# Top-k attention and a gated MLP on one core: the first 25 slots issued in an order from a table, six gates and twelve small additions moved to GpSimd

## The chip, the cores and the metric

The kernel runs on one core of a Trainium2 chip. The metric is the device time of one execution in microseconds. The core has five instruction queues that run side by side, each strictly in the order in which the program lists it: TensorE (PE; its weight loads are shown apart as PEld), VectorE (DVE), ScalarE (ACT), GpSimd (POOL) and SyncE (SP), which here issues nearly all transfers. Engines wait for each other through semaphores.

## The reference

Attention over 8 batches of 8 heads, 576 rows of 64, in which each row keeps its 32 largest scores; its output, 4608 rows of 512, goes through a dense block of width 2048 with a gate.

```python
scores = scale * np.matmul(q, k.transpose(0, 1, 3, 2))
kth = np.partition(scores, -32, axis=-1)[..., -32:-31]
scores = np.where(scores >= kth, scores, -1e9)
attn = np.exp(scores - np.max(scores, axis=-1, keepdims=True))
attn = attn / (np.sum(attn, axis=-1, keepdims=True) + 1e-09)
x = np.matmul(attn, v)            # then (B, H, S, D) -> (B*S, H*D)
h = x @ w_in
out = (h * (1.0 / (1.0 + np.exp(-1.702 * h)))) @ w_out
```

q, k and v are float32; w_in and w_out come as float64.

## The kernel before

**Slots.** The attention is cut into 144 slots of 128 rows by two heads (or four heads' last 64 rows), 18 to a batch. A slot runs through these steps, each a function of the kernel:

- `scores` (L330): eight matmuls on PE into the only score buffer in PSUM, `s_ps`. `copy_scores` (L345): ACT copies them to `sc`, of which there are four buffers.
- `pair_up` (L354): DVE writes the larger and the smaller of each two scores to `ranked`. `topk` (L374): four rounds of MAX8 and MATCH_REPLACE8 on DVE find the 32 largest. Since `pair_up` empties the score buffer together with `copy_scores`, it stands in the middle of the ranking of the slot before.
- `bounds` (L399): POOL makes `cut` and `low` from `top`. `mask` (L414) and `exps` (L422) on ACT give `pr` and the sums `den`. `invert` (L433): 1e-9 is added to `den` (on DVE up to slot 11, on POOL from slot 12, because of `n > PAIRED`), and DVE takes the reciprocal `rden`.
- The probabilities are transposed. Up to slot 9 PE does it, with a diagonal matrix `by` that POOL makes from `rden` (`divide` L443, `turn` L458). From slot 10 on POOL normalizes `pr` (L450), ACT splits it into halves of words in `sc` (`split` L486), SP writes them to `rows` in DRAM and reads them back transposed into `pt` (`turn_by_dma` L494).
- `values` (L515, L548, L566): matmuls of `v` with `pt`, 64 output rows at a time, the two heads side by side in the array; ACT copies the result to `xT`.

**Blocks.** Four slots make a block of 128 rows for the dense part; there are 36. Each is worked off in four units: `hidden` (L651) is the matmul with w_in; `tanh` (L673) is ACT's; `gate` (L685) multiplies; `combine` (L702) makes sums for the seven products that `project` (L755) multiplies with w_out. The first two blocks (`whole`) are done without such sums. `tanh(aside)` chooses the gate's engine: with `False` one DVE instruction reads the hidden values from PSUM; with `True` ACT first copies them to `h` in SBUF, and POOL takes two instructions.

**Weights.** The 32 pieces of w_in and w_out arrive as float64 and are made float32 during slots 0 to 10, by steps of `round_piece` (L136) on ACT (`size`, `sign`, `low`), DVE (`shift`) and POOL (`finish`, `pool_size`). PE gets dummy matmuls from `stay_warm` (L170) in slots with little to do.

**Order.** All order is written by hand, and the issue order of the program is each engine's order. `opening` (L907) begins; `slot` (L949) does slots 0 to 10; `filling_slot` (L1099), called by `filling` (L1138), does 11 to 20 with lists of extra work; `steady_pair` (L1175) does two slots at a time from 21 on; `last_units` (L1241) works off the dense units that are left. Loads of v are `load_v` (L208): v has one buffer, so the load for the next batch waits for the last values of this one.

Of the kernel before, what the change touches and what calls it, by code (L numbers as in the profile page):

```python
# [9 lines left out]
ALU = mybir.AluOpType  # L10
# [19 lines left out]
TO_ZERO = 2.0**-100  # L30


@with_exitstack
def kernel(
    ctx: ExitStack,
# [23 lines left out]

    nc = tc.nc

    B, H, S, D = q.shape
    C = H * D
# [23 lines left out]
    PAIRED = SETTLED + 1  # L89
    STEADY = PAIRED + 2  # L90
# [25 lines left out]
    both_banks = [ps_p.tile([P, 512], F32, name=f"po{i}") for i in range(2)]  # L116

    ident = const.tile([P, P], F32, name="ident")
    make_identity(nc, ident[:])
    win = const.tile([P, CC, DFF], F32, name="win")  # L120
    wout = const.tile([P, FC, C], F32, name="wout")

# [199 lines left out]
    N = len(slots)  # L322
    PER = N // B
    st = [{} for _ in slots]
# [83 lines left out]
    def exponentials(n, between=lambda: None):  # L408

        mask(n)  # L410
        between()
        exps(n)
# [20 lines left out]
    def invert(n):  # L433

        some = small.tile([P, 2], F32, name="some", tag="sums")
        if n > PAIRED:
            nc.gpsimd.tensor_scalar(some[:], st[n]["den"][:], 1e-9, None, op0=ALU.add)  # L437
        else:
            nc.vector.tensor_scalar_add(some[:], st[n]["den"][:], 1e-9)
        rden = st[n]["rden"] = small.tile([P, 2], F32, name="rden", tag="inverse")  # L440
        nc.vector.reciprocal(rden[:], some[:])  # L441

# [190 lines left out]
    class Block:  # L633
        def __init__(self, place, rows):
            self.place, self.rows = place, rows
            self.whole = len(blocks_seen) < WHOLE
            self.bank = 1 - len(blocks_seen) % 2
            blocks_seen.append(self)
            self.left = list(range(FC))
            if not self.whole:  # L640
                self.left = [h * (FC // 2) + 2 * u + c for u in range(4) for h in range(2) for c in range(2)]
            self.done = 0
# [30 lines left out]
    def tanh(aside):  # L673

        if to_gate:
            ph, fs, x = to_gate.pop(0)
            th = thp.tile([P, G * P], F32, name="th")
            nc.scalar.activation(th[:], ph, AF.Tanh, scale=0.851 / RAISE)
            if aside:
                h = thp.tile([P, G * P], F32, name="h", tag="th")  # L680
                nc.scalar.copy(out=h[:], in_=ph)  # L681
                ph = h[:]
            gated.append((th, ph, fs, x, aside))
# [161 lines left out]
    for n in by_slot:  # L845
        first = sum(map(len, list(by_slot.values())[:n]))
# [60 lines left out]
    def opening():  # L907

        stay_warm(8, v_tail[:, 0, :, :].rearrange("p j d -> p (j d)"))
        load("q", 0, 0, nc.sync)  # L910
        load("k", 0, 0, nc.scalar)
        for hp in range(2):
            for name in "qk":
                if hp:
                    load(name, 0, hp)
        for x in by_slot[0]:
            load_piece(x)
        prepare_first()
# [30 lines left out]
    def slot(n):  # L949

        todo = later.pop(n, [])
        for fn, args in todo:
            if fn not in (prepare, prepare_by_dma, load_piece):
                fn(*args)
        preparing = [(fn, args) for fn, args in todo if fn is prepare or fn is prepare_by_dma]
        some = [round_piece(x) for x in by_slot.get(n, [])] if n else early
        steps = {name: [piece[name] for piece in some] for name in ("size", "shift", "low")}
        last = some[-1] if len(some) > 2 else None
        if last:
            steps["size"].pop()  # L960

        def do(name, count):
            for _ in range(min(count, len(steps[name]))):
                steps[name].pop(0)()

        if n == 0:
            steps["size"].clear()
            do("low", 3)
        else:
            exponentials(n - 1, bring_all if n % 4 == 1 and n > TURNS + 1 else lambda: None)  # L970
            if n == TURNS + 1:
                stay_warm(14)
                bring_all()
            copy_scores(n + 1)
            bring_all()
            if 1 < n <= TURNS:
                turn_main(n - 2)
                turn_ends(n - 2)
            if n > TURNS + 1:
                tanh(False)  # L980
            do("size", 3)
            if n == TURNS + 1:
                do("low", 3)
                tanh(False)
        for i, op in enumerate(topk(n)):
            op()
            if i == 1:
                for _ in range(min(3, len(unfinished))):
                    finish_one()
                if last and n > 2:  # L990
                    last["pool_size"]()
            if i == (9 if n < 3 else 7):
                if n > 0:
                    divide(n - 1)
                if last and n < 3:
                    last["pool_size"]()
# [36 lines left out]
        if n > PROJECTS and may_project(2):  # L1033
            project(n == SETTLED)
        if idle:
            stay_warm(8)
        if n == SETTLED:
            turn_qk(1, 0)
        hidden()
# [59 lines left out]
    def filling_slot(n, beside, pool_ahead, behind, pool_behind, late=[]):  # L1099

        todo = later.pop(n, [])
        due = [(fn, args) for fn, args in todo if fn is prepare_by_dma]
        exponentials(n - 1)
        for fn in beside:
            fn()
        for fn in pool_ahead:
            fn()
        find(n, 8)
        for fn, args in todo:
            if fn is load_v:  # L1110
                fn(*args)
        scores(n + 2)
        if n == PAIRED:
            normalize(n - 1)
            split(n - 1)
            copy_scores(n + 2)
        else:
            copy_scores(n + 2)
            normalize(n - 1)
            split(n - 1)  # L1120
        write_all()
        for fn, args in todo:
            if fn not in (prepare_by_dma, load_v):
                fn(*args)
        turn_by_dma(n - 1)
        while turns:
            turns.pop(0)()
        for fn in pool_behind:
            fn()
        bounds(n)  # L1130
        for fn in behind + late:
            fn()
        for fn, args in due:
            fn(*args)
# [106 lines left out]
    def last_units():  # L1241
# [7 lines left out]
        project_one()  # L1249
        leave_all()  # L1250

    with tc.manual_schedule():
        opening()
        for n in range(SETTLED + 1):
            slot(n)
        filling()
        for n in range(STEADY + 8, N + 2, 2):
            steady_pair(n)
        combine()
        while ready or to_gate or gated or to_combine or to_project:  # L1260
            last_units()
        merge_some(len(merging), nc.vector)
        write_all()
# [30 lines left out]
```

## Time and profile before

| | us |
|---|---|
| median of three runs (lowest, highest) | 1379.32 (1377.34, 1382.84) |
| the profiled execution's own time | 1379.59 |
| its span | 1377.8 |
| busy: PE, DVE, ACT, POOL | 1341.2, 1286.0, 1164.1, 964.4 |
| mean granted TensorE clock | 0.992 |

The span runs from the first to the last instruction that the profiler recorded; the time is a little longer than it. Busy time is the time in which an engine had an instruction under way; for PE the ends of matmuls are modelled, and a float32 matmul shows as two records. A row of the groups gives line, engine, operation, output and inputs with their shapes, the count, then busy us, the mean of one in ns, the idle time before them and what ended it. `POOL by L448` is the instruction on POOL that writes `by` at line 448. A row of the timeline gives start, length, and what ran, with equal neighbours merged (x4 is four).

### The profile page before, as it was taken

How to read it: one execution, taken by the hardware profiler on the slowest of the kernel's cores; microseconds unless marked ns; L12 is line 12 of the kernel's file. 1: busy time of each engine (PE TensorE's matmuls, PEld its weight loads, DVE VectorE, ACT ScalarE, POOL GpSimd, SP SyncE). 2: the span in 40 equal slices, each digit the busy share in tenths (PEclk: the TensorE clock that was granted, in tenths of full speed). 3: DMA queues.
4: the chain of work that ended last, by engine and by line, in shares of the span. 5: the costliest groups of instructions: out<-in, count | busy, mean ns of one | idle time of the engine just before them, and what ended most of it. 6: DMA issues, size and time to landing. Idle time of an engine off the chain costs nothing.

```text
span 1377.8 us, 54398 instructions
## 1 busy us (share of the span) xinstructions
PE 1341.2 (97%) x22560; PEld 1205.0 (87%) x22560; DVE 1286.0 (93%) x3392; ACT 1164.1 (84%) x1930; POOL 964.4 (70%) x1758
## 2 busy tenths in 40 slices
PE   7789999999999999999999999999999999999998
PEld 5676578899999999999999999999998999999998
DVE  7999998999999999999999999999999999999912
ACT  6988887998889888988898988888888998888841
POOL 3776676777777776777777777677777777777770
PEclk8999999999999999999999999999999999999999
DMA  7551568787889786977898668988888768855640
GB/s 232 155 163 62 151 159 198 179 196 196 205 210 211 178 189 173 232 193 192 192 227 208 182 174 193 210 198 191 197 211 208 195 176 183 184 142 135 151 118 17
DMA packets 527223, 246.92 MB, mean 179 GB/s; under 512 B 458880, under 2 KB 505472, under 8 KB 526976
## 3 DMA queue, kind: packets, MB, share of 16 engines
q1 hardware_dynamic: 526544, 243.16, 71.5%
q8 instruction: 177, 2.90, 0.9%
q14 instruction: 70, 0.57, 0.1%
q10 hardware_dynamic: 432, 0.30, 0.1%
HBM read 46.01 MB, written 103.42 MB: 108 GB/s over the span
## 4 chain that ended last, share of the span: by engine, by line
PE 79%; DMA 3%; ACT 1%; issue 0%; POOL 0%; SPq 0%; DVE 0%; DVEq 0%; ACTq 0%; POOLq 0%
PE ph L662 32%; PE po L776 28%; PE o L586 10%; PE s_ps L339 9%; DMA pt<-rows 2%; DMA rows<-sc 1%; ACT pr L428 0%; ACT sc L418 0%; ACT sc L490 0%; ACT sc L350 0%; ACT halves L268 0%; ACT raws L794 0%; SPq L221 0%; POOL pr L454 0%; ACT h L681 0%
## 5 line engine op out<-in xcount | busy, mean ns | idle before, releaser
L386 DVE MAX8 top<-ranked 128x8 f32<-128x288 f32 (+1 forms) x1152 | 637.6, 596 | 0.0
L662 PE MATMUL ph<-xT,win 128*64 128x128 f32 (+1 forms) x8544 | 493.8, 273 | 0.0
L662 PEld LDWEIGHTS ph<-xT,win 128*64 128x64 f32 (+1 forms) x8544 | 469.4, 137 | 27.6 <-issue 24.1
L390 DVE MATCH_REPLACE8 ranked<-top,ranked 128x288 f32<-128x288 f32 (+1 forms) x864 | 462.4, 543 | 0.0
L490 ACT COPY sc<-pr 128x2304 uint16<-128x2304 uint16 x134 | 283.4, 2115 | 90.1 <-POOL pr L454 90.0
L454 POOL TENSOR_SCALAR pr<-pr,rden 128x576 f32<-128x576 f32 x268 | 197.9, 748 | 49.2 <-DVE rden L441 47.7
L428 ACT ACTIVATE pr<-sc,low 128x576 f32<-128x576 f32 x288 | 219.9, 769 | 0.0
L418 ACT ACTIVATE sc<-sc,cut 128x576 f32<-128x576 f32 x288 | 208.6, 779 | 4.7 <-POOL cut L404 4.7
L360 DVE TENSOR_TENSOR ranked<-s_ps,sc 128x576 f32<-128x576 f32 x286 | 201.8, 747 | 3.8 <-ACT sc L350 3.8
L776 PE MATMUL po<-raws,h 128*64 128x128 f32 x2112 | 205.3, 273 | 0.0
L776 PE MATMUL po<-wout,h 128*64 128x128 f32 x2112 | 205.3, 273 | 0.0
L350 ACT COPY sc<-s_ps 128x576 f32<-128x576 f32 x286 | 168.5, 642 | 26.9 <-PE s_ps L339 14.4
L437 POOL TENSOR_SCALAR some<-den 128x2 f32<-128x2 f32 x132 | 29.3, 222 | 221.6 <-ACT pr L428 221.4
L339 PE MATMUL s_ps<-qk_t 64*64 64x288 f32 x2304 | 177.6, 421 | 5.6 <-DVE ranked L360 4.4
L691 POOL TENSOR_TENSOR th<-th,h 128x512 f32<-128x512 f32 x134 | 171.8, 1282 | 11.2
L776 PE MATMUL po<-wout,th 128*64 128x128 f32 x2176 | 165.3, 273 | 0.0
L776 PEld LDWEIGHTS po<-raws,h 128*64 128x64 f32 x2112 | 133.8, 137 | 0.0
L776 PEld LDWEIGHTS po<-wout,h 128*64 128x64 f32 x2112 | 133.7, 137 | 0.0
L776 PEld LDWEIGHTS po<-wout,th 128*64 128x64 f32 x2176 | 127.8, 137 | 0.9 <-POOL wout L739 0.4
L339 PEld LDWEIGHTS s_ps<-qk_t 64*64 64x64 f32 x2304 | 76.2, 134 | 58.1 <-issue 14.8
L586 PE MATMUL o<-pt,v_l 128*64 128x128 f32 (+1 forms) x2240 | 124.8, 265 | 0.0
L586 PEld LDWEIGHTS o<-pt,v_l 128*64 128x64 f32 x2240 | 110.3, 137 | 10.1 <-issue 9.5
(118 smaller groups left out, 1647.5 us busy)
## 6 DMA issues: line engine op xcount, KB each, us to landing
rows<-sc SPq DMA_DIRECT2D x134, 576.0 KB, 4.0
qk_rows<-halves SPq DMA_DIRECT2D x24, 576.0 KB, 5.5
out_dram<-raws SPq DMA_DIRECT2D x68, 128.0 KB, 3.7
raws<-in_moe_w_in_dram SPq DMA_DIRECT2D x16, 512.0 KB, 5.1
raws<-in_moe_w_out_dram SPq DMA_DIRECT2D x16, 512.0 KB, 3.7
qk_l<-in_q_dram SPq DMA_DIRECT2D x28, 256.0 KB, 4.4
qk_l<-in_k_dram SPq DMA_DIRECT2D x28, 256.0 KB, 4.2
v_l<-in_v_dram SPq DMA_DIRECT2D x4, 1024.0 KB, 8.8
```

The source lines that it names most:

```text
L339: nc.tensor.matmul(ps[rows, i, c, 0:HALF], lhsT=qT[b, hps[p]][on, cols], rhs=kT[b, hps[p]][on, FIRST[i] + c * HALF : FIRST[i] + (c + 1) * ...
L360: nc.vector.tensor_tensor(out=ranked[n][:, :, c, :], in0=a, in1=b, op=op)
L386: nc.vector.max(top[:, i, 8 * r : 8 * r + 8], of(r, i))
L390: nc.vector.match_replace(to, top[:, i, 8 * r : 8 * r + 8], of(r, i), LOWEST)
L418: nc.scalar.activation(sc[:, i, :], sc[:, i, :], AF.Prelu, bias=cut[:, i : i + 1], scale=SCALE, alpha=HUGE)
L428: nc.scalar.activation(pr[:, i * S : (i + 1) * S], sc[:, i, :], AF.Exp, bias=low[:, i : i + 1], accum_out=den[:, i : i + 1],)
L454: nc.gpsimd.tensor_scalar(pr[:, i, :], pr[:, i, :], st[n]["rden"][:, i : i + 1], 1.0, op0=ALU.mult, op1=ALU.mult)
L490: nc.scalar.copy(out=halves, in_=pr[:].bitcast(U16).rearrange("p (k h) -> p h k", h=2))
L586: nc.tensor.matmul(o[s][j * D : (j + 1) * D, cols], lhsT=lhsT, rhs=rhs, start=(s, j) not in halves[:k], stop=(s, j) not in halves[k + 1 :],)
L662: nc.tensor.matmul(ph[rows, i * P : (i + 1) * P], lhsT=win[:, c, f * P + rows.start : f * P + rows.stop], rhs=xs[:, x.place, c, :], start= ...
L691: nc.gpsimd.tensor_tensor(out=th[:], in0=th[:], in1=h, op=ALU.mult)
L776: nc.tensor.matmul(both_banks[bank][y * TAIL : (y + 1) * TAIL, to * P : (to + 1) * P], lhsT=a[:, i, :], rhs=weight(w, fs[i])[:, y, :], sta ...
```

## The change

Four things are changed.

1. All engines are wrapped. While steps are collected, a call of an engine is stored and not issued; opening, slots 0 to 20 and the pairs that begin with 21 and 23 (so slots 0 to 24) become 2609 stored steps. A table `ORDER` lists these numbers once each (`2+4` is 2, 3, 4, 5), and they are issued in its order. Buffers are still handed out in the order of the functions. From pair 25 on all is issued directly, as before.
2. `tanh(False)` in slots 5 to 10 becomes `tanh(True)`: six gates of the first two blocks go from DVE to POOL, with six more copies on ACT.
3. In `invert` the addition of 1e-9 is always POOL's: that moves the ones of slots 0 to 11.
4. In `filling_slot` loads of v are stored behind the slot's split rather than ahead of its scores.

```diff
+COLLECTED = 25
+
+ORDER = """
+8 11 0+8 9 12 10 13+4 22 24+2 17 26+5 18 31 23 34 33 32 19 35 42 36 43+3 20 37 46+4 21 97 50 56+4 98 51 61+4 60
...
+2566 2579 2503 2580+8 2504 2607 2603 2588+8 2608 2605 2505 2604 2528+4 2606 2532+6 2599+2
+"""
+class Engine:
+    def __getattr__(self, name):
+        do = getattr(self.engine, name)
+
+        def step(*args, **kwargs):
+            if self.engines.collected is None:
+                do(*args, **kwargs)
+            else:
+                self.engines.collected.append(lambda: do(*args, **kwargs))
+
+        return step
...
-    nc = tc.nc
+    nc = Engines(tc.nc)
...
-        if n > PAIRED:
-            nc.gpsimd.tensor_scalar(some[:], st[n]["den"][:], 1e-9, None, op0=ALU.add)
-        else:
-            nc.vector.tensor_scalar_add(some[:], st[n]["den"][:], 1e-9)
+        nc.gpsimd.tensor_scalar(some[:], st[n]["den"][:], 1e-9, None, op0=ALU.add)
...
             if n > TURNS + 1:
-                tanh(False)
+                tanh(True)
             do("size", 3)
             if n == TURNS + 1:
                 do("low", 3)
-                tanh(False)
+                tanh(True)
...
         find(n, 8)
-        for fn, args in todo:
-            if fn is load_v:
-                fn(*args)
         scores(n + 2)
...
         for fn, args in todo:
-            if fn not in (prepare_by_dma, load_v):
+            if fn is not prepare_by_dma:
                 fn(*args)
...
+    def issue_in_order():
+
+        steps, nc.collected = nc.collected, None
...
+        for i in order:
+            steps[i]()
+
     with tc.manual_schedule():
+        nc.collected = []
         opening()
         for n in range(SETTLED + 1):
             slot(n)
         filling()
-        for n in range(STEADY + 8, N + 2, 2):
+        for n in range(STEADY + 8, COLLECTED, 2):
+            steady_pair(n)
+        issue_in_order()
+        for n in range(COLLECTED, N + 2, 2):
             steady_pair(n)
```

On PE the table mixes matmuls of different units one by one; on DVE the rankings of two slots are interleaved and `pair_up` comes earlier in them; on ACT and POOL the steps of the weights move between those of the slots. SP's list stays as it was but for one place: the load of v for batch 1 stands one `rows` transfer later.

More of the change, by code (lines that the diff above doesn't have):

```diff
@@ L30, with __init__ @@
 TO_ZERO = 2.0**-100
+COLLECTED = 25
+ORDER = """
[84 rows of a table added]
+"""
+class Engine:
+    def __init__(self, engines, engine):
+        self.engines, self.engine = engines, engine
+    def __getattr__(self, name):
[6 more added lines that the diff above has]
+        return step
+class Engines:
+    def __init__(self, nc):
+        self.collected = None
+        for name in ("tensor", "vector", "scalar", "gpsimd", "sync"):
+            setattr(self, name, Engine(self, getattr(nc, name)))
 @with_exitstack
@@ L118 @@
     ident = const.tile([P, P], F32, name="ident")
-    make_identity(nc, ident[:])
+    make_identity(tc.nc, ident[:])
     win = const.tile([P, CC, DFF], F32, name="win")
@@ L1250, in last_units @@
         leave_all()
+    def issue_in_order():
+        steps, nc.collected = nc.collected, None
+        order = list(range(len(steps)))
+        if ORDER.split():
+            order = []
+            for part in ORDER.split():
+                first, _, count = part.partition("+")
+                order += range(int(first), int(first) + int(count or 1))
+        assert sorted(order) == list(range(len(steps)))
+        for i in order:
+            steps[i]()
     with tc.manual_schedule():
+        nc.collected = []
         opening()
```

82 rows, old and new, of the table ORDER are left out of this document.

## The prediction

> **What bounds the kernel now.** I read the profile's busy times and its chain of waits first, then the busy time by stretches of time, then the instruction groups and waits of the first 263 us.
>
> ```profile
> PE 1341.2 (97%) x22560; PEld 1205.0 (87%) x22560; DVE 1286.0 (93%) x3392; ACT 1164.1 (84%) x1930; POOL 964.4 (70%) x1758
> ...
> PE 79%; DMA 3%; ACT 1%; issue 0%; POOL 0%; SPq 0%; DVE 0%; DVEq 0%; ACTq 0%; POOLq 0%
> ```
>
> Over the whole span TensorE looks like the bound and VectorE is close behind. The stretches tell where that holds. Columns are start and end, length, then busy us of PE, weight loads, DVE, ACT, POOL, then the granted clock.
>
> ```profile
> 9.00:132.80 123.80, 102.63 (x921) 81.18 (x921) 119.68 (x303) 105.25 (x208) 81.89 (x99) 0.92 0.51 160
> 132.80:262.90 130.10, 122.92 (x1738) 97.67 (x1736) 122.62 (x328) 109.70 (x185) 93.49 (x151) 1.00 0.67 164
> ...
> 262.90:1304.70 1041.80, 1040.56 (x18622) 953.07 (x18619) 1025.63 (x2713) 925.06 (x1499) 756.76 (x1444) 1.00 0.79 191
> 1304.70:1377.80 73.10, 67.16 (x1228) 66.23 (x1224) 17.15 (x48) 21.58 (x39) 31.17 (x57) 0.99 0.28 73
> ```
>
> From 262.9 us to 1304.7 us PE is busy 1040.56 of 1041.80 us: that stretch is full, and the change does not enter it. Slots 0 to 10 lie in the first stretch, 11 to 24 in the second (slot 11's ranking begins with the second MAX8 of the row below); DVE is the fullest engine of the first (97%), and PE and DVE are level in the second (94%).
>
> ```profile
> 132.10 1.48 DVE L386 MAX8 top<-ranked 128x8 f32<-128x576 f32 x3
> ```
>
> Next, the edge between what is reordered and what is not, on PE and DVE.
>
> ```profile
> 262.94 0.61 PE L776 MATMUL po<-wout,th 128*64 128x128 f32 x8
> ...
> 280.57 0.61 PE L776 MATMUL po<-wout,th 128*64 128x128 f32 x8
> ```
>
> ```profile
> 260.82 2.13 DVE L386 MAX8 top<-ranked 128x8 f32<-128x576 f32 x4
> ...
> 265.29 1.41 DVE L360 TENSOR_TENSOR ranked<-s_ps,sc 128x576 f32<-128x576 f32 x2
> ...
> 273.93 1.41 DVE L360 TENSOR_TENSOR ranked<-s_ps,sc 128x576 f32<-128x576 f32 x2
> ```
>
> PE repeats every 17.63 us (280.57 - 262.94) a pair of slots; DVE needs 8.64 us a slot (273.93 - 265.29), 17.28 a pair, so it can follow but hardly catch up. Slot 25's ranking begins halfway through the x4 row, at about 262. From there the end is 1377.8 - 262.9 = 1114.9 us away, PE-bound and unchanged. The whole change is therefore worth the shift of the edge at 262.9 us, and nothing else.
>
> **The change, part by part.** First what leaves DVE: six gates (one instruction each) and twelve additions of 1e-9. These are the DVE groups of the first stretch, then of the first 262.2 us; the last columns are count, busy us, mean ns, idle before and its cause.
>
> ```profile
> L158 DVE TENSOR_SCALAR win<-win 128x512 uint32<-128x512 uint32 x16 | 7.4, 511 | 0.0
> L439 DVE TENSOR_SCALAR some<-den 128x2 f32<-128x2 f32 x10 | 6.7, 667 | 3.5 <-ACT pr L428 3.5
> L158 DVE TENSOR_SCALAR wout<-wout 128x512 uint32<-128x512 uint32 x16 | 5.8, 416 | 0.0
> L693 DVE SCALAR_TENSOR_TENSOR th<-th,po 128x512 f32<-128x512 f32 x6 | 4.1, 676 | 0.0
> ```
>
> ```profile
> L360 DVE TENSOR_TENSOR ranked<-s_ps,sc 128x576 f32<-128x576 f32 x50 | 35.3, 747 | 3.2 <-ACT sc L350 3.2
> ...
> L439 DVE TENSOR_SCALAR some<-den 128x2 f32<-128x2 f32 x12 | 7.0, 582 | 4.2 <-ACT pr L428 4.2
> ...
> L441 DVE RECIPROCAL rden<-some 128x2 f32<-128x2 f32 x24 | 3.8, 160 | 4.1 <-POOL some L437 3.7
> ```
>
> In the first stretch DVE loses 6.7 + 4.1 = 10.8 us of work, and the 3.5 us in which it stood waiting for the additions' input can be filled, since the table puts other ranking steps there. Its floor becomes 119.68 - 10.8 = 108.9 us against 123.8 now.
>
> Second, what arrives elsewhere. POOL's rows for the same operations, and ACT's copy `h`, which this kernel makes for every gate on GpSimd:
>
> ```profile
> L691 POOL TENSOR_TENSOR th<-th,h 128x512 f32<-128x512 f32 x11 | 14.1, 1282 | 0.9
> L690 POOL TENSOR_SCALAR th<-th 128x512 f32<-128x512 f32 x11 | 6.8, 621 | 0.0
> L404 POOL TENSOR_SCALAR cut<-top 128x4 f32<-128x4 f32 x24 | 5.4, 226 | 50.0 <-DVE top L386 50.0
> L437 POOL TENSOR_SCALAR some<-den 128x2 f32<-128x2 f32 x12 | 2.7, 223 | 16.0 <-ACT pr L428 15.9
> ```
>
> ```profile
> L681 ACT COPY h<-po 128x512 f32<-128x512 f32 x4 | 2.4, 596 | 0.0
> ```
>
> POOL gets 6 x (0.621 + 1.282) = 11.4 us of gates and 10 x 0.223 = 2.2 us of additions in the first stretch: 81.89 + 13.6 = 95.5 us. ACT gets 6 x 0.596 = 3.6 us: 105.25 + 3.6 = 108.9 us. So after the change ACT's work in slots 0 to 10 is as long as DVE's floor. That is the term that decides the first stretch: it can be no shorter than 108.9 us, and it lasts 108.9 divided by the share that the fullest engine reaches. The nearest rows for such a share are ACT's 925.06 of 1041.80 (88.8%) in the steady stretch, where nothing pressed it, and 100%. The first gives 122.6 us, a gain of 1.2; the second a gain of 14.9. I take the middle, 94.4%, because DVE holds 97% in this stretch today with a simpler order, and ACT's weight preparation has steps (for w_out) that the table may let slip into slots 11 and 12: 115.3 us, **a gain of 8.5 us**.
>
> The Trainium skill, GPSIMD Engine Reference, section "Engine selection", speaks against this part: elementwise work belongs on VectorE, GpSimd being about 2x slower for two inputs. The rows agree: 0.621 + 1.282 = 1.90 us a gate on POOL against 0.676 on DVE. By that rule the move is a loss wherever POOL is the fullest engine, and the sum is then that of the POOL rival below, 1387 us; by the stretch's rows POOL ends at 95.5 us beside floors of 108.9, and the sum stays.
>
> Third, DVE's remaining work may get slower beside a fuller POOL. Rows of one kind at different moments:
>
> ```profile
> 28.48 1.08 DVE L158 TENSOR_SCALAR win<-win 128x512 uint32<-128x512 uint32 x3
> ...
> 38.66 1.86 DVE L158 TENSOR_SCALAR win<-win 128x512 uint32<-128x512 uint32 x3
> ...
> 55.34 1.29 DVE L439 TENSOR_SCALAR some<-den 128x2 f32<-128x2 f32 x1 [0.43 <-ACT pr L428]
> ...
> 66.60 0.17 DVE L439 TENSOR_SCALAR some<-den 128x2 f32<-128x2 f32 x1 [0.20 <-ACT pr L428]
> ```
>
> The same shift takes 0.36 or 0.62 us, the same addition 0.17 or 1.29. The 32 shifts take 13.2 us, 1.7 over 32 x 0.36. POOL's share in the stretch goes from 66% to 95.5 / 115.3 = 83%; in proportion the excess grows by 0.4 us, between 0 and 32 x 0.26 - 1.7 = 6.6. I take **a loss of 0.5 us**. The Trainium skill, GPSIMD Engine Reference, section "Specifications", says that GpSimd shares its SBUF interfaces with VectorE's two-port modes, which agrees with these rows; the term stands without it.
>
> Fourth, the order in slots 11 to 24. DVE idles 130.10 - 122.62 = 7.5 us there and PE 7.2; neither loses work, so 7.5 us is the most to be had and 0 the least unless waits are added. One of the waits is a transfer: loading v of the next batch stands ahead of a slot's scores in SP's queue.
>
> ```profile
> 226.58 0.59 SPq L210 DMA_DIRECT2D v_l<-in_v_dram  x1
> 227.22 1.49 SPq L221 DMA_DIRECT2D v_e<-in_v_dram  x2
> 228.76 1.14 SPq L492 DMA_DIRECT2D rows<-sc  x1
> ```
>
> ```profile
> 237.00 1.18 ACT L350 COPY sc<-s_ps 128x576 f32<-128x576 f32 x2 [4.63 <-DMA rows<-sc]
> ```
>
> The copy of scores needs the buffer that the rows transfer empties; that was issued 2.2 us late behind v and took 8.2 us to land beside it (228.76 to 236.9). DVE stood for 3.2 us behind this copy (its L360 row above). In the changed program v's three loads stand after that rows transfer. SP's queue is otherwise the same list. If the next transpose is late instead, PE's values two slots on have cover: PE has dense units to run. I count the 3.2 us as gone, and 1.0 of the other 4.3 us (the 3.7 us of waits for POOL's addition stay hard to hide, since POOL is in order too): **a gain of 4.2 us**, between 0 and 7.5.
>
> Fifth, PE's own order. Values and dense matmuls are now mixed one by one. Ten half-width matmuls run in pairs, 75.11 - 73.87 = 1.24 us:
>
> ```profile
> 73.87 1.09 PE L526 MATMUL o<-pt,v_l 128*64 128x128 f32 x16
> 74.79 0.39 PE L526 MATMUL o<-pt,v_e 128*64 128x128 f32 x4
> 75.11 3.84 PE L662 MATMUL po<-xT,win 128*128 128x128 f32 x32
> ```
>
> In the changed program 33 runs of half-width matmuls have an odd length, none before; each leaves half an array idle for 1.24 / 10 = 0.124 us, 4.1 us in all, nearly all in slots 2 to 15. PE idles 123.8 - 102.6 = 21.2 us in the first stretch, which covers those there; about a third falls where PE is level with DVE, a **loss of 0.6 us** after PE's 7.2 us of idle there, from 0 to 4.1. The 60 warm-up matmuls stay 60 and only move; the granted clock of 0.92 in this stretch may fall, and the same 21.2 us cover that. Recording the steps adds no instruction.
>
> The sum: 8.5 - 0.5 + 4.2 - 0.6 = 11.6 us off the edge. The profiled execution took 1379.59 us (span 1377.8), 0.3 over the median of 1379.32, so I forecast **1368.0 us**. The ends of the terms give 1379.6 - 14.9 - 7.5 = 1357.2 and, with all at their worst, 1379.6 - 1.2 + 6.6 + 4.1 = 1389.
>
> **The rivals.**
>
> *The table nearly reaches the floor.* For it: DVE's and ACT's floors agree at 108.9, DVE's in the second stretch is 122.6, and DVE today has 97% in the hardest place. Against: no stretch but the steady one shows two engines above 97% together. 14.9 + 5 = 20 off: 1360 us.
>
> *The gain is eaten by waits in the order.* Every engine runs its list strictly, so a step that is late holds all that stands behind it. ACT stays at 88.8% (gain 1.2) and the second stretch keeps only the transfer's 3.2: 1375 us. For it: PE waits for the `by` matrices up to 3.5 us at a time already:
>
> ```profile
> PE tp L468 <- POOL by L448: 7.0, 4, 3.5
> ```
>
> Against: mixed lists give each wait other work ahead of it.
>
> *Slower, by POOL in slots 5 to 10.* Its gates stand among `cut`, `some` and `by`, on which masks, reciprocals and transposes wait; POOL also waits 50.0 us for `top` in the L404 row, time it cannot use unless the lists fit. If it packs no better than in the steady stretch, 756.76 / 1041.80 = 72.6%, the first stretch lasts 95.5 / 0.726 = 131.5 us, 7.7 longer: 1387 us. It decides from 95.5 / 123.8 = 77% downwards. Against: those waits are on `top`, where later work can now stand; the ranking itself needs no POOL result.
>
> That nothing is changed is no case: the built lists of all five engines differ, SP's only at v's loads.
>
> **How the numbers follow.** About 0.5% (6.9 us) is what a measurement of this kernel can tell from no change. Forecast (1361 to 1372): 0.47; floor (under 1361): 0.17; gain eaten (1372 to 1386): 0.23, of which 0.02 still falls under 1372.4; POOL or another mishap in the lists (over 1386): 0.13. Faster 0.47 + 0.17 + 0.02 = 0.66, same 0.21, slower 0.13. The range goes from the floor's end, 1357.5, to 1381, inside the eaten case; some 0.16 lies above it and 0.02 below. The likeliest case's own range is 1361 to 1372.
>
> **What would show it.** Slot 25's first MAX8 on DVE at about 250.5 instead of 262, and slot 11's at about 124 instead of 132.8; PE's period of 17.63 us unchanged after it. In the first stretch ACT above 92% busy, POOL near 83%. No wait for `rows` at v's load. DVE has no `some` and no gate. The forecast is wrong if ACT stays below 90% in slots 0 to 10, if POOL's `cut` or `by` shows up as what DVE's or ACT's waits end on, or if the steady part starts with PE out of step and the period is longer.

## The result, and the profile after

The changed kernel takes 1384.47 us (median; 1380.70 to 1387.35) against 1376.96 us (1374.66 to 1382.84) for the kernel before, measured beside it: a ratio of 1.0053, 95% interval 1.0040 to 1.0067. It is slower by half a per cent. The forecast was 1368.0 us, and the range ended at 1381.

The page of the changed kernel, first the busy times, then the shares of the chain that ended last:

```profile
PE 1361.2 (98%) x22560; PEld 1211.3 (87%) x22560; DVE 1274.8 (92%) x3374; ACT 1166.3 (84%) x1936; POOL 976.4 (71%) x1782
...
PE 94%; DMA 2%; ACT 2%; issue 1%; POOL 1%; DVE 0%; SPq 0%; DVEq 0%; ACTq 0%; POOLq 0%
```

DVE lost 11.2 us of work (1286.0 before), as the change says. PE has the same 22560 records and is busy 20 us longer (1341.2 before). The same work takes PE more time: that is the first sign. The stretches, with the columns of the prediction's (length, then PE, weight loads, DVE, ACT, POOL, granted clock):

```profile
66.90:132.80 65.90, 65.11 (x546) 48.70 (x548) 60.69 (x161) 56.50 (x111) 51.00 (x69) 1.00 0.42 130
...
9.00:132.80 123.80, 111.74 (x889) 83.03 (x891) 109.87 (x290) 102.06 (x202) 86.32 (x112) 0.92 0.51 159
132.80:269.60 136.80, 134.31 (x1782) 102.52 (x1784) 124.14 (x329) 118.88 (x201) 104.36 (x165) 0.99 0.66 155
269.60:1311.40 1041.80, 1040.38 (x18620) 953.06 (x18618) 1022.72 (x2705) 921.74 (x1495) 753.45 (x1441) 1.00 0.80 191
```

The last row is the steady part, unchanged. Between 66.9 and 132.8 us PE is now full, 65.11 of 65.90 us. The kernel before, in the same stretch:

```profile
66.90:132.80 65.90, 58.37 (x536) 46.97 (x536) 63.05 (x156) 55.39 (x106) 46.64 (x56) 0.97 0.40 122
```

It got through nearly as many matmuls of the same kinds (536 records against 546; 134 of half width against 160) in 58.37 us. Then the edge, on PE and on DVE (all stored steps have the line of the wrapper, L134; steps from pair 25 on have L132):

```profile
129.94 0.45 DVE L134 MAX8 top<-ranked 128x8 f32<-128x288 f32 x1
```

```profile
269.63 0.61 PE L132 MATMUL po<-wout,th 128*64 128x128 f32 x8
```

```profile
267.13 0.81 DVE L132 MAX8 top<-ranked 128x8 f32<-128x288 f32 x2
```

The first row is the 89th MAX8: a slot has eight of them, so eleven slots' worth lie before it. It comes at 129.94 us, about 2.9 earlier than before (132.8). It measures the work done: slot 11's own first MAX8 comes at 124.41, since the table interleaves two slots and slot 10's last comes only at 132.05 (132.10 before). Slot 25's ranking begins at 267.13 instead of about 262.2, so from the 89th MAX8 to there it takes 137.2 us where it took 129.4. Pair 25's first product starts at 269.63 instead of 262.94. These 6.7 us are the whole difference of the spans (1384.5 - 1377.8); behind the edge both kernels need 1114.9 us. What PE does in the full part (start, length, output and inputs, equal neighbours merged; two records are one float32 matmul):

```profile
96.34 0.39 PE L134 MATMUL po<-xT,win 128*128 128x128 f32 x2
96.66 0.43 PE L134 MATMUL o<-pt,v_l 128*64 128x128 f32 x2
97.02 0.49 PE L134 MATMUL po<-xT,win 128*128 128x128 f32 x2
97.44 0.65 PE L134 MATMUL o<-pt,v_l 128*64 128x128 f32 x6
98.02 0.71 PE L134 MATMUL po<-xT,win 128*128 128x128 f32 x4
```

`128*128` and `128*64` are the parts of the array that a matmul uses: the whole, or half of its columns. From one half-width matmul to the full one behind it are 0.36 us (97.02 - 96.66), and from the full to the half 0.32 to 0.42. In the kernel before, runs of values gave 0.124 us a matmul (the prediction's row of ten in 1.24 us), and the hidden matmuls behind them took 3.84 / 16 = 0.24. Last, the waits before the edge that touch the prediction's steps (engine, what it did, what it waited for, us, times, longest):

```profile
POOL raws L134 <- ACT raws L134: 18.3, 5, 12.0
DVE rden L134 <- POOL some L134: 14.9, 10, 2.4
DVE ranked L134 <- ACT sc L134: 11.8, 8, 3.1
...
POOL win L134 <- DMA raws<-in_moe_w_in_dram: 5.2, 1, 5.2
...
ACT sc L134 <- DMA rows<-sc: 3.2, 1, 3.2
...
PE o L134 <- DMA pt<-rows: 2.2, 2, 2.0
```

DVE's wait for POOL's addition went from 3.7 to 14.9 us, its wait for the copied scores from 3.2 to 11.8.

### The profile page after: what moved, and what is told of

Its sections match the earlier page's. It is cut to its first block, busy times and chain, and to the rows that moved or that the text cites. A ratio compares the mean times of both kernels' runs of the same rounds, so it can differ in the third digit from the quotient of the medians.

```text
span 1384.5 us, 54392 instructions
## 1 busy us (share of the span) xinstructions
PE 1361.2 (98%) x22560; PEld 1211.3 (87%) x22560; DVE 1274.8 (92%) x3374; ACT 1166.3 (84%) x1936; POOL 976.4 (71%) x1782
## 4 chain that ended last, share of the span: by engine, by line
PE 94%; DMA 2%; ACT 2%; issue 1%; POOL 1%; DVE 0%; SPq 0%; DVEq 0%; ACTq 0%; POOLq 0%
PE ph L132 32%; PE po L132 28%; PE o L132 9%; PE s_ps L132 9%; PE po L134 7%; PE o L134 2%; PE tp L134 2%; DMA pt<-rows 2%; PE s_ps L134 2%; PE ph L134 1%; ACT sc L134 1%; ACT pr L134 0%; DMA rows<-sc 0%; POOL raws L134 0%; ACT raws L134 0%
## 5 line engine op out<-in xcount | busy, mean ns | idle before, releaser
L132 DVE MAX8 top<-ranked 128x8 f32<-128x288 f32 (+1 forms) x952 | 526.8, 596 | 0.0
L132 PE MATMUL ph<-xT,win 128*64 128x128 f32 x8064 | 464.3, 273 | 0.0
L132 PEld LDWEIGHTS ph<-xT,win 128*64 128x64 f32 x8064 | 441.2, 137 | 25.9 <-issue 21.9
L132 DVE MATCH_REPLACE8 ranked<-top,ranked 128x288 f32<-128x288 f32 x714 | 382.2, 543 | 0.0
L132 ACT COPY sc<-pr 128x2304 uint16<-128x2304 uint16 x120 | 253.7, 2115 | 88.8 <-POOL pr L132 88.8
L132 POOL TENSOR_SCALAR pr<-pr,rden 128x576 f32<-128x576 f32 x240 | 176.7, 746 | 42.7 <-DVE rden L132 42.7
L132 PE MATMUL po<-raws,h 128*64 128x128 f32 x2000 | 194.3, 273 | 0.0
L132 PE MATMUL po<-wout,h 128*64 128x128 f32 x2000 | 194.3, 273 | 0.0
L132 ACT ACTIVATE pr<-sc,low 128x576 f32<-128x576 f32 x240 | 183.5, 771 | 0.0
L132 ACT ACTIVATE sc<-sc,cut 128x576 f32<-128x576 f32 x240 | 174.3, 782 | 0.1
L132 POOL TENSOR_SCALAR some<-den 128x2 f32<-128x2 f32 x120 | 26.4, 220 | 204.7 <-ACT pr L132 204.7
L132 DVE TENSOR_TENSOR ranked<-s_ps,sc 128x576 f32<-128x576 f32 x236 | 166.7, 748 | 2.0 <-ACT sc L132 2.0
L132 POOL TENSOR_TENSOR th<-th,h 128x512 f32<-128x512 f32 x123 | 157.5, 1280 | 10.3
L132 PE MATMUL po<-wout,th 128*64 128x128 f32 x2064 | 156.6, 273 | 0.0
L132 ACT COPY sc<-s_ps 128x576 f32<-128x576 f32 x234 | 137.8, 642 | 19.9 <-PE s_ps L132 8.7
L132 PE MATMUL s_ps<-qk_t 64*64 64x288 f32 x1872 | 140.5, 415 | 0.0
L132 PEld LDWEIGHTS po<-raws,h 128*64 128x64 f32 x2000 | 126.4, 137 | 0.0
L132 PEld LDWEIGHTS po<-wout,h 128*64 128x64 f32 x2000 | 126.3, 137 | 0.0
L132 PEld LDWEIGHTS po<-wout,th 128*64 128x64 f32 x2064 | 121.2, 137 | 0.0
L132 PE MATMUL o<-pt,v_l 128*64 128x128 f32 (+1 forms) x2144 | 120.8, 267 | 0.0
L132 PEld LDWEIGHTS o<-pt,v_l 128*64 128x64 f32 x2144 | 106.6, 137 | 9.8 <-issue 9.3
L132 POOL TENSOR_TENSOR h<-th 128x128 f32<-128x128 f32 x248 | 113.6, 458 | 0.3
```

Of the source, the lines that this page charges most:

```text
L132: do(*args, **kwargs)
```

## The experiments

Three theories were set against each other. **A**: PE's own order, the many changes between full and half width, makes PE the bound. **B**: waits in the table's own lists on VectorE and GpSimd, of which one late step on POOL near the start was tried. **C**: the moves to GpSimd themselves. All ratios are to the kernel before on the chip of that run.

**The moves without the table.**

```diff
 ORDER = """
-8 11 0+8 9 12 10 13+4 22 24+2 ...
+0+2609
 """
```

> The changed kernel with its steps issued in the order in which the functions list them: the table is out, the six gates and twelve additions on GpSimd and the later load of v stay. Theory A (broken runs: the table cuts PE's half-width matmuls into pieces between full-width ones, each change of width costs PE time, and PE is the bound from about 70 us on): runs are whole again, PE has idle time again in the first 263 us, and the time is 1368 to 1376. Theory B (waits in the table's lists on DVE and POOL): also 1368 to 1376, DVE's wait for some under 5 us. Theory C (the moves to GpSimd cost the time, the table is innocent): 1382 to 1390.

Measured: 1389.24 us, ratio 1.0075 (1.0058 to 1.0092). So the moves (and v's later load, which stays in) cost time in the written order, as C said; the 1368 to 1376 expected under A and under B did not come. Whether the table recovers a part of it is not shown: the changed kernel's 1.0053 lies below, but the intervals overlap. The two moves were then made one at a time in the kernel before.

**The six gates alone.**

```diff
             if n > TURNS + 1:
-                tanh(False)
+                tanh(True)
...
                 do("low", 3)
-                tanh(False)
+                tanh(True)
```

> The kernel before with only the six gates moved to GpSimd, no table, additions on DVE, v's load where it was. Theory C1 (in written order it is the additions that cost, since each stands in POOL's list behind steps of 1.3 us and DVE waits for it): DVE loses 4.1 us of work, POOL has room, 1373 to 1379. Theory C2 (the gates cost, by filling POOL in slots 5 to 10): 1385 to 1392.

Measured: 1382.47 us, ratio 1.0015 (1.0004 to 1.0026), between the two ranges expected. DVE's groups from 9.0 to 132.8 us show why the 4.1 us that leave DVE bring nothing:

```profile
L158 DVE TENSOR_SCALAR wout<-wout 128x512 uint32<-128x512 uint32 x15 | 12.6, 889 | 0.0
L158 DVE TENSOR_SCALAR win<-win 128x512 uint32<-128x512 uint32 x16 | 7.5, 523 | 0.0
```

A shift of w_out, 416 ns before, takes 889 beside the gates on POOL: 7.1 us more for 15 of them, above the 4.1 saved. In this trace each shift during which one of the gates' instructions runs takes 0.64 to 1.51 us, and each during which GpSimd runs nothing takes 0.41 to 0.42.

**The twelve additions alone.**

```diff
-        if n > PAIRED:
-            nc.gpsimd.tensor_scalar(some[:], st[n]["den"][:], 1e-9, None, op0=ALU.add)
-        else:
-            nc.vector.tensor_scalar_add(some[:], st[n]["den"][:], 1e-9)
+        nc.gpsimd.tensor_scalar(some[:], st[n]["den"][:], 1e-9, None, op0=ALU.add)
```

> The kernel before with only the twelve additions of 1e-9 moved to GpSimd. Theory C1: from slot 2 on DVE waits about 2.7 us a slot for some at its reciprocal, ten times, against 7.0 us of additions and 4.2 us of waits for den that go: 1386 to 1396. Theory C2: 1370 to 1378.

Measured: 1391.51 us, ratio 1.0075 (1.0059 to 1.0091). One line of the waits up to the edge, then POOL and DVE around one addition:

```profile
DVE rden L438 <- POOL some L436: 26.8, 14, 2.8
```

```profile
83.76 0.64 POOL L156 TENSOR_SCALAR wout<-raws 128x512 f32<-128x512 f32 x1
84.48 0.22 POOL L436 TENSOR_SCALAR some<-den 128x2 f32<-128x2 f32 x1
```

```profile
84.73 0.17 DVE L438 RECIPROCAL rden<-some 128x2 f32<-128x2 f32 x1 [2.16 <-POOL some L436]
```

The addition takes 0.22 us, but on POOL it stands behind the steps of the weights, and DVE, also in order, stands for 2.16 us before the reciprocal. This is C, and nearly all of the loss in the written order: 26.8 us of waits (3.7 before) for the 7.0 us of additions that DVE was spared.

**The additions back on VectorE, the table kept.**

```diff
-        nc.gpsimd.tensor_scalar(some[:], st[n]["den"][:], 1e-9, None, op0=ALU.add)
+        if n > PAIRED:
+            nc.gpsimd.tensor_scalar(some[:], st[n]["den"][:], 1e-9, None, op0=ALU.add)
+        else:
+            nc.vector.tensor_scalar_add(some[:], st[n]["den"][:], 1e-9)
```

> The changed kernel with the twelve additions of slots 0 to 11 back on DVE, at the same places of the table. Theory B: DVE's wait for some (14.9 us) goes for slots 0 to 11, partly replaced by waits for den; 1380 to 1384. Theory A: DVE is not the bound in this part, its waits are covered: 1383 to 1387. Theory C: about 1380.

Measured: 1386.64 us, ratio 1.0047 (1.0031 to 1.0064), no different from the changed kernel. Two lines of its waits up to the edge:

```profile
DVE some L134 <- ACT pr L134: 9.1, 8, 2.6
DVE rden L134 <- POOL some L134: 5.5, 3, 3.2
```

The wait for POOL falls from 14.9 us to 5.5, DVE waits 9.1 us for the additions' own input instead, and nothing is gained. So in the changed kernel the loss is not at this wait.

**PE's runs joined.** In the table, the ten matmuls of each call of `values`, and the last two of each transpose, are issued together at the place where the last of them stood. Nothing is moved ahead of what it needs, and the lists of the other four engines stay as they were. An excerpt of the table (values are 1339 to 1358):

```diff
-1339+8 1458 1325 1457 1222 1347 1460 1348 1409 1378 1361 1317 1349+8 1406 ... 1320 1357+2
+1458 1325 1457 1222 1460 1339+10 1409 1378 1361 1317 1406 ... 1320 1349+10
```

> The changed kernel with one edit of the table: the ten half-width matmuls of a slot's values, and the two of its last transpose, are issued together where the last of them stood; all other lists are the table's. Runs of half-width matmuls go from 72 to 48, odd ones from 33 to 4. Theory A: PE saves about 24 round trips of 0.24 us and 29 half matmuls of 0.06 to 0.12 us, 7 to 9 us: 1375 to 1378. Theory B: 1382 to 1386, since no list but PE's is changed.

Measured: 1373.51 us, ratio 0.9963 (0.9951 to 0.9975): 11.0 us below the changed kernel's median (0.90% by the ratios, 12.4 us), and faster than the kernel before. That is what A said, and more than its 1375 to 1378; B's 1382 to 1386 did not come. The stretches, and then the 89th MAX8 and slot 25's first on DVE:

```profile
66.90:132.80 65.90, 65.63 (x610) 51.86 (x611) 64.33 (x170) 62.07 (x124) 54.62 (x73) 1.00 0.41 130
132.80:253.20 120.40, 116.89 (x1640) 89.48 (x1642) 115.31 (x303) 107.38 (x178) 96.99 (x153) 1.00 0.74 171
9.00:132.80 123.80, 111.21 (x969) 86.25 (x968) 116.62 (x306) 109.73 (x220) 92.40 (x119) 0.93 0.51 159
```

```profile
123.37 0.45 DVE L131 MAX8 top<-ranked 128x8 f32<-128x288 f32 x1
...
253.18 0.81 DVE L129 MAX8 top<-ranked 128x8 f32<-128x288 f32 x2
```

PE is as full as in the changed kernel, but 610 records fit where 546 did, and DVE, ACT and POOL are fuller too. The work of eleven slots is done by 123.37 us, near the 124 of the prediction. The clock explains little of the gain: the changed kernel's granted clock is 0.79 in the 8 us from 248 us (its row stands in the last section), an estimated loss of 8 x 0.21 = 1.7 us, and the clocks of the stretches in these rows and the changed kernel's differ by 0.01 at most.

**The opposite: runs cut in the kernel before.** In slots 6 to 9, where both have work, `values` and `hidden` are collected and issued in turns, one matmul each. Nothing else is changed.

```diff
...
+            while ours or theirs:
+                for some_of in (ours, theirs):
+                    if some_of:
+                        args, kwargs = some_of.pop(0)
+                        nc.tensor.matmul(*args, **kwargs)
...
```

> The kernel before with, in slots 6 to 9, the ten half-width matmuls of values and the sixteen full-width ones of hidden issued in turns, one of each, where a slot has both. Theory A: a turn of one half-width and one full-width matmul takes 0.55 to 0.7 us, where the runs take 0.12 + 0.22 = 0.34; about 3 us more PE work in each such slot, half of it covered by PE's idle time there; 1378 to 1386. Without a price for the change of width a turn takes 0.34 to 0.40 us and the time is 1376 to 1382.

Measured: 1386.2 us in the one profiled run (span 1384.4 against 1377.8). It is a single execution; the kernel before took 1377.70 to 1382.59 us beside it. PE's timeline, and the busy times of the second stretch:

```profile
83.86 0.43 PE L1061 MATMUL o<-pt,v_l 128*64 128x128 f32 x2
84.22 0.49 PE L1061 MATMUL po<-xT,win 128*128 128x128 f32 x2
84.64 0.43 PE L1061 MATMUL o<-pt,v_l 128*64 128x128 f32 x2
```

```profile
66.90:132.80 65.90, 63.59 (x479) 45.80 (x479) 58.07 (x149) 51.80 (x100) 47.12 (x57) 1.00 0.42 122
```

One turn takes 0.78 us (84.64 - 83.86). In runs the same two matmuls take about 0.34: each is two records, and in runs records start 0.112 us apart at full width and 0.055 on average at half width (the last section has these). So a turn costs 0.44 us more, 0.22 for each of its two changes of width.

That price holds two things, since each half-width matmul of a turn also stands alone. In the changed kernel there are turns in which pairs are whole:

```profile
141.89 0.44 PE L134 MATMUL o<-pt,v_l 128*64 128x128 f32 x4
142.26 0.49 PE L134 MATMUL ph<-xT,win 128*128 128x128 f32 x2
...
142.90 0.44 PE L134 MATMUL o<-pt,v_l 128*64 128x128 f32 x4
```

The pair takes 0.37 us to the next start (142.26 - 141.89), the lone matmul above 0.36 (84.22 - 83.86): alone, it takes as long as two. From one pair to the next are 1.01 us, for two half-width and two full-width matmuls that take 0.67 in runs. So a change costs (1.01 - 0.67) / 2 = 0.17 us where pairs stay whole, and a lone half-width matmul about 0.1 more, near the 0.124 of the prediction.

From 66 to 140 us this trace has 67 changes between full and half width, the kernel before 12; 55 / 2 x 0.44 = 12.1 us of PE, of which its idle 7.5 us (65.90 - 58.37) cover a part. PE's busy time grew by 11.0 us (1352.2 against 1341.2), the span by 6.6. The changed kernel has 95 such changes and 24 runs with an odd number of half-width matmuls from 66 us to its edge, the one with joined runs 50 and 1: by the prices of 0.17 and 0.124 an estimated 45 x 0.17 + 23 x 0.124 = 10.5 us, of the 11.0 to 12.4 measured.

**One POOL step later.** One conversion of a piece of w_in (step 183) is moved behind slot 0's addition (step 179).

```diff
-185 183 172 186 212 204+4 ... 225+8 214 258 257 208 179 189
+185 172 186 212 204+4 ... 225+8 214 258 257 208 179 183 189
```

> The changed kernel with one step of the table moved: POOL's first step on a piece of w_in, which stood between cut and low of slot 0 and waited 5.2 us for its transfer, now stands behind the addition for slot 0. Theory B: the first exponentials come 4 to 5 us earlier, the waits of slots 1 to 4 behind them shrink, and the time is 1379 to 1381. Theory A: PE's full stretch begins earlier only by what slots 0 to 4 gain, at most 2 us: 1382 to 1385.

Measured: 1381.68 us, ratio 1.0014 (1.0005 to 1.0024). POOL in the changed kernel, and then with the step moved:

```profile
21.28 0.23 POOL L134 TENSOR_SCALAR cut<-top 128x4 f32<-128x4 f32 x1
26.67 0.66 POOL L134 TENSOR_SCALAR win<-raws 128x512 f32<-128x512 f32 x1 [5.16 <-DMA raws<-in_moe_w_in_dram]
27.29 0.20 POOL L134 TENSOR_TENSOR low<-cut 128x2 f32<-128x2 f32 x1
```

```profile
21.68 0.23 POOL L134 TENSOR_SCALAR cut<-top 128x4 f32<-128x4 f32 x1
21.99 0.19 POOL L134 TENSOR_TENSOR low<-cut 128x2 f32<-128x2 f32 x1
```

In the changed kernel the second bound of slot 0 (`low`) stands behind a step that waits 5.16 us for its weights to land; without that it comes at 21.99 instead of 27.29. B is worth 1384.47 - 1381.68 = 2.8 us by the medians, 0.39% or 5.4 us by the ratios.

**Both edits together**, run on two chips.

> Both edits of the table together: runs of half-width matmuls joined, and POOL's first step on a piece of w_in behind the addition of slot 0. If the two causes are apart, the gains add (12 and 4 us off the changed kernel): 1368 to 1371. If the late piece only mattered because PE was full, 1373 to 1375.

> The program with joined runs and the piece behind once more, on the same chip as the next two. If the 1369.65 us of its four runs stands for it, 1368 to 1371. If its executions fall in two groups by the pause before 235 us and the clock after it, as those with the additions back on VectorE did (1370 and 1375), the median lies between: 1371 to 1374.

Measured: 1369.65 us, ratio 0.9917 (0.9901 to 0.9933) on the first, 1372.14 us, ratio 0.9955 (0.9940 to 0.9970) on the second. The changed kernel's ratio less both single gains, 1.0053 - 0.0090 - 0.0039 = 0.9924, lies within the first interval and outside the second. So on the first chip the two gains add up; on the second the program is no better than joined runs alone (0.9963, 0.9951 to 0.9975), and that the late step still costs anything there is not shown. It is faster than the kernel before; whether by 0.5% or by 0.8%, the two chips leave open.

**The moves where the order has been mended.** From that program, the additions or the gates go back to VectorE; each gate (one instruction again, its copy gone) stands in the table ahead of the next unit's first hidden matmul. Each was run on two chips, the second time beside the program itself.

```diff
-                tanh(True)
+                tanh(False)
```

> The program with joined runs and the piece behind (1369.65 us, 0.9917 of before), with the twelve additions of 1e-9 back on VectorE at the same places of the table. If the move of the additions still costs time once TensorE has its runs back (the wait for POOL, 3.6 us in all on rden in that program), this gives about 3 us: 1365 to 1368. If the table hides it (TensorE full from 67 to 254 us, as its 65.61 busy of 65.9 says), the additions' own 6.7 us on VectorE are hidden as well: 1368 to 1371. If VectorE is the bound there, they come back in part: 1372 to 1376.

> The twelve additions back on VectorE, beside the program above on one chip. If their move is worth something where the table orders the work, 3 to 5 us more than the run above; if it is hidden there, within 1.5 us of it.

> The same program with the six gates back on VectorE (one instruction each instead of two on POOL and a copy on ACT), each standing in the table ahead of the next unit's first hidden matmul. If the gates' move to POOL brings time where TensorE is full, this is slower by up to their 4.1 us: 1371 to 1375. If TensorE alone is the bound there, nothing is lost: 1367 to 1371, and less if the shifts on VectorE get shorter beside a freer POOL.

> The six gates back on VectorE, beside the two above on one chip. If their move is worth something, 4 to 7 us more than the first; if it is hidden, within 1.5 us of it.

Measured with the additions back: 1373.87 us, ratio 0.9956 (0.9941 to 0.9971), and beside the program 1374.40 us, 0.9965 (0.9953 to 0.9976) against its 0.9955. That is no difference the intervals can tell, and the 4 us between the first two medians were a comparison of two chips. With the gates back: 1376.13 us, 0.9976 (0.9963 to 0.9989), and beside the program 1375.96 us, 0.9985 (0.9975 to 0.9994), above its 0.9940 to 0.9970. So the gates' move gains 0.3%, some 4 us, against gates at this one place in the table; that of the additions was not shown to gain or lose.

**The place of v's loads.** In the same program, the three loads of v for batch 1 go one place forward in SP's queue (ahead of `rows<-sc`, as in the kernel before) or one place back (behind the transpose `pt<-rows`).

```diff
 forward:
-rows<-sc  v_l  v_e  v_e  pt<-rows
+v_l  v_e  v_e  rows<-sc  pt<-rows
 back:
-rows<-sc  v_l  v_e  v_e  pt<-rows
+rows<-sc  pt<-rows  v_l  v_e  v_e
```

> The program with joined runs and the piece behind, with the three loads of v for batch 1 moved one place forward in SP's queue: ahead of the rows transfer, where the kernel before had them. If that place is worth the 3.2 us counted in the fourth step, this is slower: 1371 to 1374. If the stall only changes its victim (there TensorE waited 2.3 us for the transposed pt behind v, at 233.5 us, and its clock fell behind such a pause in some executions), nothing or a little is gained: 1366 to 1370.

> The same with the loads of v one place later: behind the transpose of pt, which then does not share the transfer engines with the 1 MB of v. If the wait for pt is what costs, 2 to 4 us are gained: 1365 to 1368. If TensorE then waits for v instead (7.5 us to land), the same or up to 2 us more: 1369 to 1372.

Measured: 1373.94 us, ratio 0.9967 (0.9954 to 0.9980), and 1373.91 us, 0.9966 (0.9952 to 0.9980); both within the span of the program's own intervals on its two chips. Neither was run beside the program itself. The traces show who waits in turn. First the forward place: ACT waits for the rows, then PE, behind DVE, for room for the scores.

```profile
ACT sc L131 <- DMA rows<-sc: 6.1, 1, 6.1
```

```profile
233.06 1.74 PE L131 MATMUL s_ps<-qk_t 64*64 64x288 f32 x16 [4.83 <-DVE ranked L131]
```

Then the place back, where PE waits for v itself; the second row is a stretch: length, PE, granted clock, share and GB/s of DMA:

```profile
235.59 0.93 PE L131 MATMUL o<-pt,v_e 64*64 64x64 f32 x16 [5.60 <-DMA v_e<-in_v_dram]
```

```profile
236.00:242.00 6.00, 6.00 (x109) 0.58 0.38 85
```

In between, the place that the changed kernel chose (here on the second chip), PE waits for the transposed `pt`:

```profile
233.21 0.57 PE L131 MATMUL o<-pt,v_e 64*64 64x64 f32 x16 [2.42 <-DMA pt<-rows]
```

```profile
236.00:242.00 6.00, 6.00 (x116) 1.00 0.74 194
```

The transfers hold something up in each of the three orders; what changes is who stands.

## Why the prediction was wrong, step by step

**The fifth step failed: PE's own order.** It priced only the runs with an odd number of half-width matmuls, 33 x 0.124 = 4.1 us, and counted 0.6 of them. That price fits the rows, in which a lone half-width matmul takes as long as two. What the step put at nothing is the change between full and half width, 0.17 us even where pairs stay whole: the changed kernel has 95 from 66 us to its edge, the kernel before 18, an estimated 77 x 0.17 = 13.1 us. With the 4.1 that is some 17 of the 20.0 us by which PE is busier. Joining the runs gave back 11.0 us or more. The cover that the step named, 21.2 us of PE idle in slots 0 to 10, was also not where it was needed: from 66.9 to 132.8 us PE had 7.5 us, and the changed kernel has 0.8. The prediction looked for PE's idle time in the stretch as a whole, and the unpriced cost met the half of it in which PE had little.

**The first step's size stands once PE's runs are joined, but not its bound.** It said 8.5 us by slot 11. By the 89th MAX8 the changed kernel shows 2.9 (132.8 to 129.94), the one with joined runs 9.4 (132.8 to 123.37); by slot 10's last MAX8 they show 0.1 and 6.6. The step took ACT, at 94.4%, as the fullest engine. With joined runs ACT has 109.73 of 123.80 us (89%) in the whole stretch; from 66.9 to 132.8 us it has 62.07 of 65.90 (94%), but PE has 65.63, and PE sets the pace. That the size fits is in part luck. That the weight steps for w_out may slip past slot 10, as it feared, is in the trace of the changed kernel (10 of 16 shifts of w_out are done by 132.8 us), but that is not what bounded it. Its statement that a gate's move is worth time holds in the table's order with joined runs (some 4 us) and not in the written one, where contention with the shifts took it.

**The third step** took 0.5 us for slower shifts. In the changed kernel the 16 shifts of w_in have a mean of 438 ns (511 before) and the 10 of w_out 510 (416): 12.1 us for the 26, where at the old means they take 12.3. Nothing was lost there, within its range of 0 to 6.6. The upper end, 6.6 us, is what the gates alone met in the written order (7.1 us). The Trainium skill, SBUF — State Buffer, section "SBUF: two separate sides", says the pair of ports that VectorE and GpSimd share is an exclusive lock held for a whole instruction; a shift at 889 ns beside GpSimd instructions of 1.3 us agrees with that.

**The fourth step failed too: the order in slots 11 to 24.** It said 4.2 us less. With PE's runs joined the part from the 89th MAX8 to slot 25's first takes 129.8 us (123.37 to 253.18) against 129.4, no gain; counted from slot 10's last MAX8 it gains 2.4. In the changed kernel it takes 137.2, at least in part for the reason of the fifth step. Its 3.2 us for the transfer of v did not go away: ACT still waits 3.2 us for `rows`, and PE 2.0 for `pt`, the very transposition whose lateness the step called covered. It was not covered: PE stands at those values, and its list has nothing else ahead of them. Moving v ahead or behind made no difference that these runs show.

**The rivals.** The time came out nearest to the rival on the other side, 1387 us, but not by its mechanism: it said that GpSimd, packed at 72.6%, becomes the bound in slots 5 to 10. By that rival, any share of POOL below 77% makes the kernel slower. POOL has 86.32 of 123.80 us (70%), but with PE's runs joined it has 92.40 (75%), also below, and that kernel is faster than the one before: the share is not what decides. PE has 65.11 of 65.90 us (99%) from 66.9 to 132.8 us. The "gain eaten by waits" is a part: the late POOL step cost 2.8 us or more in the table as it was. No rival said that PE becomes the bound of its own making.

**What would show it.** Slot 11's first MAX8 at 124 and slot 25's at 250.5 were the signs of the forecast. The first came, at 124.41 us, but only because two slots' rankings are interleaved; by the work done it is 129.94, and slot 25's at 267.13 denies the forecast. One sign of being wrong was right: ACT stays below 90% in slots 0 to 10 (102.06 of 123.80 us, 82%), and POOL is at 70%, not near 83%. The unchanged tail (1114.9 us) was right. "POOL's `cut` or `by` as what DVE or ACT end on" was the wrong sign to look for: PE's busy time against its count of records was the one that told.

## What to carry to other kernels

When an order is rewritten on TensorE, count the changes between matmuls of different array width on each side and price each with a measured pair, before looking at any idle time; keep matmuls of one width in runs, and half-width ones in pairs, even if one could fill a gap earlier. An engine's idle time covers a cost only in the part of the stretch where both lie. A small operation moved to another in-order queue costs what stands ahead of it there, and a reordering that takes one wait off a loaded transfer queue hands it to the next in line.

## What the runs showed of the hardware that was not expected

- A change between full-width and half-width matmuls costs about 0.17 us where half-width ones come in pairs: two of each take 1.01 us with two changes, 0.67 in runs. A half-width matmul alone takes as long as a pair (0.36 and 0.37 us). Start to start, in the changed kernel, records are 0.205 us apart from full to half against 0.112 from full to full (medians), and 0.203 from half to full against 0.055 on average from half to half, where the two of a pair start 0.007 apart and the next pair 0.10 later.
- A shift on VectorE of 128x512 took 416 ns before, and 889 on average beside six GpSimd gates more.
- Pauses of PE before the edge can slow what follows. With the additions back on VectorE, the row of the pause and the stretch behind it:

```profile
234.69 0.82 PE L131 MATMUL o<-pt,v_e 64*64 64x64 f32 x16 [3.68 <-DMA pt<-rows]
```

```profile
236.00:242.00 6.00, 6.00 (x102) 0.60 0.47 102
```

After 3.68 us of pause the granted clock is 0.60 for the next stretch of 6 us, and 0.58 after the 5.60 us above, but 1.00 after 2.42. The Trainium skill, TensorE: Matmul & The Clock Gate, section "Why this matters for your kernels", advises no idle gaps over about 3 us, which these three agree with. Two other rows do not fit it. The first is the changed kernel's:

```profile
247.48 0.57 PE L134 MATMUL o<-pt,v_e 64*64 64x64 f32 x16 [2.00 <-DMA pt<-rows]
```

```profile
248.00:256.00 8.00, 8.00 (x150) 0.79 0.44 114
```

The second is from the additions back on VectorE, the run beside the program:

```profile
236.51 0.57 PE L131 MATMUL o<-pt,v_e 64*64 64x64 f32 x16 [3.50 <-DMA pt<-rows]
```

```profile
236.50:242.50 6.00, 5.99 (x146) 1.00 0.55 132
```

The pause of 2.00 us is the shortest of the five, and the clock falls to 0.79 just before the edge; the one of 3.50 us is followed by 1.00. So the length of a pause alone does not settle it, and what does was not tried.
